# Chunk inverses of groups 0 to 5 from 16 by 16 blocks, with fillers for lone stages and a higher fill limit

## The chip, the cores and the metric

The kernel runs on one core of one Trainium2 chip. The metric is the device time in microseconds of one execution, median of several runs. A core has five engines that work side by side and wait for each other by semaphores: TensorE (PE in the profile; its weight loads are PEld), VectorE (DVE), ScalarE (ACT), GpSimd (POOL) and SyncE (SP), which issues the DMAs. TensorE writes to PSUM, eight banks of 128 partitions by 512 fp32 numbers.

## The reference

Delta-rule attention over 4 batches, 8 heads, 768 steps, head size 48, and then a gated MLP with a mixing matrix over the sequence:

```python
for t in range(S):
    y[:, :, t] = einsum('bhd,bhde->bhe', q[:, :, t], state)
    v_old = einsum('bhde,bhd->bhe', state, kt)
    state = state + bt * einsum('bhd,bhe->bhde', kt, vt - v_old)
h = relu(x @ w_in); u, v = h[..., :512], h[..., 512:]
v_n = (v - mean(v)) / sqrt(var(v) + 1e-6)
out = (u * (einsum('ts,bsd->btd', w_spatial, v_n) + b_spatial)) @ w_out
```

## The kernel before, in words

**Chunks and stages.** The sequence is cut into 12 chunks of 64 steps per batch: 48 chunk stages in an order written in `step_order` (all of batch 0, then batch 1, then two batches in turn). Each treats 8 heads, two by two on the upper and lower 64 partitions. Within a chunk the recurrence is solved in closed form, which needs the inverse of a 64 by 64 unit triangular matrix for each head. Four stages make a group, so 12 groups hold 384 inverses.

**Making an inverse.** For a group, `kk` multiplies keys with keys on TensorE and masks the product into `ta` on VectorE; `bounce` writes `ta` to DRAM (`ad`), and the diagonal blocks come back with one block per partition (`la`). There VectorE eliminates row by row, one multiply (into `prod`) and one add (into `w`, held in a PSUM tile `pw`) per row. Groups 1 to 11 do that for 32 by 32 blocks (`load_la`, `lanes`: 30 rows, 60 VectorE instructions, lines 670 and 677), and the result returns over DRAM (`wd`) into `ta`. Group 0 does it for 16 by 16 blocks (`lanes16`: 14 rows, 28 instructions, lines 1181 and 1188, all in an SBUF buffer `ub`); `widen` then makes 32 by 32 inverses of them: a transpose on VectorE (line 1208), 16 small matmuls (line 1215), a masked copy on ScalarE, 16 small matmuls (line 1226), four ScalarE copies, for each stage of the group. The step from 32 to 64 is taken for every stage by `step_t` (transpose into `tn`) and `step_ef` (two stage matmuls named e and f here, one on the diagonal quadrants).

**The chain of a stage.** `step_ab`: a (keys times state) and b (inverse times corrected values), followed on VectorE by `us`; `step_c`: the state's update, followed on VectorE by `st`; then the next stage's a, followed by `kv`. `step_qk` and `step_d` make the output. Each of these TensorE stages is 8 small fp32 matmuls on quarters of the array (the profile shows 16 records), of kind "anti" or "diag" by the quarters it uses. Two stages of different kinds can be interleaved and run at the same time, in two PSUM banks.

**The MLP.** Matmuls of 256, 384 or 512 columns in four task kinds (v, u, g, o), which become possible as chunks are done; the mixing over the sequence (g) needs all of a batch.

**What sets the order.** All engines' queues are written ahead by a planner, `Line`. It keeps an estimated time for each engine and picks the next operation by readiness and due time, with costs that are constants of the code. Where its TensorE would idle, `keep_warm` adds matmuls of a matrix of ones (256 columns, line 1282) as long as the columns of the last 3.4 us stay under `FILL` (5000). Where a stage has no partner, `fake` adds a filler stage of the other kind, made of `mpos` matrices, if the same sum is under `FAKE` (5500) and a bank is free. Nothing reads the fillers' results.

Of the kernel before, what the change touches and what calls it, by code (L numbers as in the profile page):

```python
# [15 lines left out]
CH = 64  # L16
# [3 lines left out]
G = 4  # L20
# [19 lines left out]
HOLD = 1.0  # L40
PAIR = 1.0
LOW = 3600
HOT = 3050
FILL = 5000
FAKE = 5500


def step_order():
# [196 lines left out]
def delta_rule_gated_mlp(  # L245
# [113 lines left out]
    class Slots:  # L359
# [12 lines left out]
        def ready_for(self, kind):  # L372
            f = self.fit(kind)
            return f[0][0] if f else None

        def ready_both(self):
# [270 lines left out]
    def load_la(g):  # L647
        d = due(4 * g - 7)
        src = ad_g[g].rearrange("j h n t -> (h n) j t")
        for blk in range(2):  # L650
            for par in range(2):
                l0, r0 = par * 64 + blk * 32, blk * 32
                t = yield dma(at(("ad", g), ("lanes", g - 2) if g > 2 else None), d, 4.2)
                nc.sync.dma_start(out=las[g % 2][l0 : l0 + 32], in_=src[:, r0 : r0 + 32, r0 : r0 + 32])
        done["la", g] = t

    def lanes(g):
# [2 lines left out]
        w = pws[g % 2].rearrange("p (i t) -> p i t", t=32)  # L660
        for par in range(2):
            pr = rows_t(par)
            t = yield act(at(("la", g), ("wo", g - 2) if g > 2 else None), d, 512)
            nc.scalar.copy(out=w[pr], in_=la[pr, par::2, :])  # L664
        for j in range(1, 31):
            n = (j + 1) // 2
# [8 lines left out]
            )  # L675
            t = yield dve(on(t), d, n * m)
            nc.vector.tensor_add(out=w[:, :n, j + 1 : 32], in0=w[:, :n, j + 1 : 32], in1=pr)  # L677
        done["lanes", g] = t
# [4 lines left out]
        t = yield act(both(on(t), at(("wd", g - 1) if g > 1 else None)), d, 512)  # L683
# [13 lines left out]
        done["T", g] = t  # L697


    def prev(s, n=1):  # L700
# [29 lines left out]
            done["S", s] = 0.0  # L730

    def step_t(s):
        done["t", s] = yield dve(at(("T", s // G) if s >= G else ("T", 0, s), ("e", s - 2) if s >= 2 else None), due(s - 1.1), 128)
        nc.vector.transpose(out=tns[s % 2], in_=t_of(s)[:, :, 0:32])

    def step_ef(s):
# [422 lines left out]

    extra = []  # L1160

    def lanes16():
        d = due(-6)
        buf = ubs[2]
        la = buf[:, 0:256].rearrange("p (j t) -> p j t", t=16)
        w = buf[:, 256:512].rearrange("p (j t) -> p j t", t=16)
        pt = buf[:, 512:768]
        pi = buf[:, 768:1024].rearrange("p (s u t) -> p s u t", u=NU, t=16)
        src = ad_g[0].rearrange("j h n t -> (h n) j t")
        sq = [(slice(k * 32, k * 32 + 32), src[:, k * 16 : k * 16 + 16, k * 16 : k * 16 + 16]) for k in range(4)]  # L1170
        for p, x in sq:
            t = yield dma(at(("ad", 0)), d, 2.5)
            nc.sync.dma_start(out=la[p], in_=x)
        done["la16"] = t
        t = yield act(on(t), d, 256)
        nc.scalar.copy(out=w, in_=la)
        for j in range(1, 15):
            m = 15 - j
            pr = pt[:, : j * m].rearrange("p (a b) -> p a b", b=m)
            t = yield dve(on(t), d, j * m)  # L1180
            nc.vector.tensor_tensor(
                out=pr,
                in0=w[:, :j, j : j + 1].broadcast_to([128, j, m]),
                in1=la[:, j, j + 1 : 16].unsqueeze(1).broadcast_to([128, j, m]),
                op=ALU.mult,
            )
            t = yield dve(on(t), d, j * m)
            nc.vector.tensor_add(out=w[:, :j, j + 1 : 16], in0=w[:, :j, j + 1 : 16], in1=pr)
        t = yield dve(on(t), d, 16)
        nc.vector.memset(w.rearrange("p i t -> p (i t)")[:, 0:256:17], 1.0)  # L1190
        for p, x in sq:
            t1 = yield dma(on(t), d, 2.8)
            nc.sync.dma_start(out=x, in_=w[p])
        ta = ta_of(0)
        for k, (a, b) in enumerate(((0, NU), (NU, G * NU))):
            for h in range(2):
                t = yield dma(on(t1), d, 2.8)
                nc.sync.dma_start(out=flat(0)[rows_t(h), a:b], in_=ad_g[0][:, h, a:b])
            done["back", k] = t
        for s in range(G):  # L1200
            line.spawn(widen(s, buf, pi))

    def widen(s, buf, pi):
        d = due(-5 + s)
        ta = ta_of(0)
        tr = buf[:, s % 2 * 256 : s % 2 * 256 + 256].rearrange("p (u t) -> p u t", t=CH)
        t = yield dve(at(("back", min(s, 1)), ("wp", s - 2) if s > 1 else None), d, 256)
        nc.vector.transpose(out=tr.rearrange("p u t -> p (u t)"), in_=ta[:, s].rearrange("p u t -> p (u t)"))
        t = yield Op("PE", 0.7, 1.0, both(on(t), pm_s.ready), d, "full", 150)
        p = pm_s.take()  # L1210
        pp, px = (p[1][:, o : o + 64].rearrange("p (u t) -> p u t", t=16) for o in (0, 64))
        for u in range(NU):
            for q in range(4):
                r, c = q * 32, q % 2 * 32
                nc.tensor.matmul(
                    pp[r : r + 32, u], ta[r : r + 16, s, u, c : c + 32], tr[r : r + 16, u, c : c + 16],
                    start=True, stop=True,
                )
        done["wp", s] = t
        t = yield act(on(t), d, 64, 1)  # L1220
        nc.scalar.mul(out=pi[:, s], in_=pp, mul=hm)
        t = yield Op("PE", 0.45, 0.75, on(t), d, "full", 150)
        for u in range(NU):
            for q in range(4):
                r, c = q * 32, q % 2 * 32
                nc.tensor.matmul(
                    px[r : r + 16, u], pi[r : r + 32, s, u], ta[r : r + 32, s, u, c + 16 : c + 32],
                    start=True, stop=True,
                )
        for q in range(4):  # L1230
            r, c = q * 32, q % 2 * 32
            t = yield act(on(t), d, 64)
            nc.scalar.copy(out=ta[r : r + 16, s, :, c + 16 : c + 32], in_=px[r : r + 16])
        pm_s.give(p, t)
        done["T", 0, s] = t

    def load_beta():
        done["ball"] = yield dma(now, due(-11.5))
# [2 lines left out]
    def load_bias():  # L1241
        r = slice(0, 66)
        x = ubs[2][:, 0:256]
        t = yield pool(at(("T", 0, G - 1)), due(2), 256)
        nc.gpsimd.memset(x, 0.0)
        for j in range(3):
            t = yield dma(on(t), due(2))
# [24 lines left out]
    def steps(s):  # L1272
        for f in (load_kv, step_t, step_ef, step_ab, step_c, step_qk, step_d):
# [113 lines left out]
```

## Time and profile before

| | us |
|---|---|
| median of 3 runs | 563.35 (563.08 to 565.36) |
| profiled execution | 559.02 |
| its span, first to last instruction | 557.3 |
| busy: TensorE, VectorE, ScalarE, GpSimd | 509.1, 355.2, 216.9, 140.7 |
| mean granted TensorE clock | 0.941 |

The slices of the page show when the engines are busy (tenths; 40 slices of 13.9 us) and what clock TensorE was granted:

```profile
PE 5965797978979999899999999999999999999997
DVE 4899978776977988478989894683135241134210
PEclk9777586897999999899999999999999999999999
```

TensorE is busy throughout the second half; in the first ten slices it has gaps and part of the time half clock, and VectorE is busy for most of the first 24 slices. Fillers count as busy time of TensorE. The median of the runs is 4.3 us above the profiled execution.

### The profile page before, as it was taken

The page shows a single profiled execution, that of the slowest core. Times are in us where ns is not written, and L with a number is a line of the kernel's source. Part 1 is how long each engine was busy: PE and PEld are TensorE (multiplying, and loading weights), DVE is VectorE, ACT ScalarE, POOL GpSimd, SP SyncE. Part 2 cuts the span into 40 slices and gives each one's busy share as a digit, 9 for nine tenths or more (in the row PEclk, how much of TensorE's full clock was granted, in tenths as well). Part 3 has the DMA queues.
Part 4 walks back from the last instruction along what each step waited for, and adds up shares of the span by engine and source line. Part 5 has one row for each costly group of instructions (what it writes and reads, how often), then busy time and mean ns, then how long its engine had stood idle before and what let it go on. Part 6 is the DMA issues. An engine that isn't in the chain of part 4 may idle for free.

```text
span 557.3 us, 22530 instructions
## 1 busy us (share of the span) xinstructions
PE 509.1 (91%) x9605; PEld 460.0 (83%) x9605; DVE 355.2 (64%) x1436; ACT 216.9 (39%) x536; POOL 140.7 (25%) x210
## 2 busy tenths in 40 slices
PE   5965797978979999899999999999999999999997
PEld 5855786867867879798987789989987999999997
DVE  4899978776977988478989894683135241134210
ACT  3222524544625535242235465422165441137111
POOL 5525224555425441402314252310001000000000
PEclk9777586897999999899999999999999999999999
DMA  8688378495759754786875727343014010100011
GB/s 241 163 179 163 88 186 220 113 259 104 181 158 191 187 135 91 177 219 146 204 133 79 204 73 173 112 142 62 29 35 133 8 36 29 35 18 16 1 42 44
DMA packets 134256, 67.03 MB, mean 120 GB/s; under 512 B 105894, under 2 KB 123532, under 8 KB 134156
## 3 DMA queue, kind: packets, MB, share of 16 engines
q1 hardware_dynamic: 134156, 65.60, 47.8%
q8 instruction: 75, 1.23, 0.9%
q14 instruction: 25, 0.20, 0.1%
HBM read 50.11 MB, written 15.17 MB: 117 GB/s over the span
## 4 chain that ended last, share of the span: by engine, by line
PE 65%; DVE 16%; DMA 7%; issue 4%; ACT 3%; SPq 3%; POOL 0%; DVEq 0%; ACTq 0%
PE pt L438 22%; PE pm L1044 12%; PE pw L1044 6%; PE pm L1012 6%; PE pm L946 5%; PE pm L1099 5%; PE pw L1099 3%; DVE prod L670 3%; DVE pw L677 3%; DMA kv<-in_kv_t 2%; DMA la<-ad 2%; PE pm L1282 2%; PE pw L946 2%; PE pw L1012 1%; DMA ad<-ta 1%
## 5 line engine op out<-in xcount | busy, mean ns | idle before, releaser
L670 DVE TENSOR_TENSOR prod<-pw,la 128x96 f32<-128x96 f32 (+10 forms) x330 | 78.3, 241 | 13.4 <-ACT pw L664 8.8
L677 DVE TENSOR_TENSOR pw<-pw,prod 128x96 f32<-128x96 f32 (+9 forms) x330 | 81.1, 249 | 4.6
L719 POOL TENSOR_TENSOR kv<-kv,cn 128x192 f32<-128x192 f32 x48 | 24.9, 519 | 159.4 <-DMA kv<-in_kv_t 93.1
L1044 PE MATMUL pm<-wsp_h,vh 128*128 128x256 f32 x192 | 57.0, 297 | 0.0
L1044 PE MATMUL pm<-wsp_l,vh 128*128 128x256 f32 x192 | 54.2, 282 | 0.6 <-issue 0.6
L1044 PE MATMUL pm<-wsp_h,vl 128*128 128x256 f32 x192 | 54.0, 281 | 0.0
L438 PE MATMUL pt<-kv,st 48*64 48x64 f32 x768 | 53.8, 232 | 0.0
L438 PE MATMUL pt<-aq,us 64*64 64x64 f32 x768 | 52.0, 227 | 0.8 <-issue 0.8
L438 PEld LDWEIGHTS pt<-kv,st 48*64 48x64 f32 x768 | 43.3, 142 | 3.2 <-DVE ta L630 1.5
L1080 ACT CAST gh<-tmp 128x512 fp32r<-128x512 f32 x24 | 14.8, 619 | 76.0 <-DVE tmp L1061 76.0
L438 PEld LDWEIGHTS pt<-aq,us 64*64 64x64 f32 x768 | 43.5, 142 | 1.0 <-issue 1.0
L1282 PE MATMUL pm<-ones 128*128 128x256 f32 x215 | 40.6, 339 | 3.2 <-ACT ones L282 2.5
L438 PE MATMUL pt<-ta,pi 64*64 64x32 f32 x768 | 36.2, 235 | 5.1 <-issue 3.9
L595 POOL TENSOR_TENSOR mc<-mpos,cn 128x256 f32<-128x256 f32 x46 | 28.3, 628 | 43.1 <-DVE cn L583 24.8
L438 PE MATMUL pt<-kv 48*64 48x64 f32 x768 | 36.0, 233 | 3.2 <-issue 2.2
L438 PEld LDWEIGHTS pt<-kv,ta 64*64 64x64 f32 x768 | 30.2, 145 | 9.8 <-issue 3.2
L438 PEld LDWEIGHTS pt<-st,kv 48*64 48x64 f32 x704 | 26.9, 141 | 13.8 <-issue 3.7
L1282 PEld LDWEIGHTS pm<-ones 128*128 128x128 f32 x215 | 33.8, 231 | 5.3 <-ACT ones L282 2.5
L868 ACT ACTIVATE xs<-pt 112x256 f32<-112x256 f32 x48 | 18.3, 381 | 50.7 <-PE pt L438 40.1
L1044 PEld LDWEIGHTS pm<-wsp_h,vh 128*128 128x128 f32 x192 | 36.4, 190 | 1.6
L438 PE MATMUL pt<-kv,ta 64*64 64x48 f32 x768 | 35.9, 233 | 1.9 <-DVE kv L779 0.5
L1044 PEld LDWEIGHTS pm<-wsp_h,vl 128*128 128x128 f32 x192 | 36.6, 190 | 0.6 <-issue 0.6
(182 smaller groups left out, 1488.2 us busy)
## 6 DMA issues: line engine op xcount, KB each, us to landing
kv<-in_kv_t SPq DMA_DIRECT2D x48, 456.0 KB, 4.5
ad<-ta SPq DMA_DIRECT2D x24, 256.0 KB, 4.5
la<-ad SPq DMA_DIRECT2D x44, 128.0 KB, 4.1
out<-ob SPq DMA_DIRECT2D x24, 192.0 KB, 1.9
k<-in_kv_t SPq DMA_DIRECT2D x20, 224.0 KB, 3.6
knn<-in_k_nat SPq DMA_DIRECT2D x10, 384.0 KB, 3.9
wd<-w SPq DMA_DIRECT2D x22, 128.0 KB, 3.9
ta<-wd SPq DMA_DIRECT2D x44, 64.0 KB, 3.5
```

Source lines behind the costliest of these rows:

```text
L438: return lambda: nc.tensor.matmul(*a, **dict(dict(start=True, stop=True), **k))
L595: (nc.vector if t in (0, 2) else nc.gpsimd).tensor_tensor(out=mc, in0=mall, in1=cns[t // G][:, t % G, 1].unsqueeze(2).broadcast_to([128, N ...
L670: nc.vector.tensor_tensor(out=pr, in0=w[:, :n, j : j + 1].broadcast_to([128, n, m]), in1=la[:, j, j + 1 : 32].unsqueeze(1).broadcast_to([1 ...
L677: nc.vector.tensor_add(out=w[:, :n, j + 1 : 32], in0=w[:, :n, j + 1 : 32], in1=pr)
L719: nc.gpsimd.tensor_tensor(out=v, in0=v, in1=cns[s // G][:, s % G, 0].unsqueeze(2).broadcast_to([128, NU, HD]), op=ALU.mult)
L868: nc.scalar.mul(out=xt[0:112, :, qt * 64 : qt * 64 + 64], in_=psl(held[0][1], CH)[0:112], mul=-1.0)
L946: nc.tensor.matmul(p[1], a[:, kt, ts], w[:, kt, DH:], start=(n == 0), stop=(n == 3 * NK - 1))
L1012: nc.tensor.matmul(pu[:, k], w[:, kt, d0 : d0 + 128], a[:, kt], start=(n == 0), stop=(n == 3 * NK - 1))
L1044: nc.tensor.matmul(pg[:, k], v[:, d0 : d0 + 128], w[:, si, ts], start=(n == 0), stop=False)
L1080: nc.scalar.copy(out=gh[:, hs], in_=gt)
L1099: nc.tensor.matmul(p[1][:, :DM], a[:, dd, ts], w[:, dd], start=(n == 0), stop=(n == 3 * ND - 1))
L1282: nc.tensor.matmul(free[0].rearrange("p (n t) -> p n t", t=128), ones, ones.unsqueeze(1).broadcast_to([128, 2, 128]), start=True, stop=True,)
```

## The change

Three things change together.

1. Groups 0 to 5 take their inverses from 16 by 16 blocks (`LG = 6`). `lanes16` and `widen` become functions of the group. `w` now lies in PSUM (`pw`), is copied to an SBUF tile by ScalarE and goes back to DRAM from there; `la`'s buffer also serves as the scratch space of `widen`, so the loads of group g wait until group g-2 has been widened (`laf`). From group 1 on, `widen` treats two stages at once (`WN = 2`), and it takes its PSUM bank from the four of the stages (`st_s`) instead of the MLP's (`pm_s`).
2. `FAKE` goes from 5500 to 99999: every lone stage takes a filler stage along where a bank is free.
3. `FILL` goes from 5000 to 7500.

```diff
+LG = 6
+WN = 2
+WP, WX = 0.35, 0.25
-FILL = 5000
-FAKE = 5500
+FILL = 7500
+FAKE = 99999
...
-                t = yield dma(at(("ad", g), ("lanes", g - 2) if g > 2 else None), d, 4.2)
+                t = yield dma(at(("ad", g), ("laf", g - 2) if g > 1 else None), d, 4.2)
...
-    def lanes16():
-        d = due(-6)
-        buf = ubs[2]
+    def lanes16(g):
+        d = due(4 * g - 3.5 if g else -6)
+        flat_l = las[g % 2].rearrange("p j t -> p (j t)")
+        la = flat_l[:, 0:256].rearrange("p (j t) -> p j t", t=16)
+        pt = prods[g % 2]
+        w = pws[g % 2][:, 0:256].rearrange("p (j t) -> p j t", t=16)
+        wc = ws.rearrange("p i t -> p (i t)")[:, g % 2 * 256 : g % 2 * 256 + 256].rearrange("p (j t) -> p j t", t=16)
...
         for p, x in sq:
-            t = yield dma(at(("ad", 0)), d, 2.5)
+            t = yield dma(at(("ad", g), *free), due(4 * g - 7) if g else d, 4.2 if g else 2.5)
             nc.sync.dma_start(out=la[p], in_=x)
...
+        t = yield act(both(on(t), at(("wd", g - 2) if g > 1 else None)), d, 256)
+        nc.scalar.copy(out=wc, in_=w)
...
+    def widen(g, s, n):
+        d = due(4 * g - 2 + s if g else -5 + s)
+        ta = ta_of(g)[:, s : s + n]
+        area = las[g % 2].rearrange("p j t -> p (j t)")
...
-        t = yield Op("PE", 0.7, 1.0, both(on(t), pm_s.ready), d, "full", 150)
-        p = pm_s.take()
+        t = yield Op("PE", WP * n, WP * n + 0.3, both(on(t), st_s.ready_plain), d, "full", 150)
+        p = st_s.take_plain()
...
-        if g:
+        if g >= LG:
             line.spawn(load_la(g))
             line.spawn(lanes(g))
         else:
-            line.spawn(lanes16())
+            line.spawn(lanes16(g))
```

The planner turns this into another order on every engine. In counts of the whole program: TensorE's `ones` fillers 253 before, 468 now; `mpos` filler matmuls 232 and 472; widening matmuls 128 and 768; VectorE's row steps of the inverses 688 and 528. In the rows below the numbers behind names tell buffers of the same kind apart.

VectorE before, between the inverse of group 2 and stage 8's `us` (`pw_210` is group 3's array, `ta_179` group 2's inverse):

```order
L670 TENSOR_TENSOR prod_184<-pw_210,la_182 128x110
L677 TENSOR_TENSOR pw_210<-pw_210,prod_184 128x11x10
L670 TENSOR_TENSOR prod_184<-pw_210,la_182 128x99
L734 STREAM_TRANSPOSE tn_175<-ta_179 128x128
L677 TENSOR_TENSOR pw_210<-pw_210,prod_184 128x11x9
L734 STREAM_TRANSPOSE tn_176<-ta_179 128x128
L670 TENSOR_TENSOR prod_184<-pw_210,la_182 128x96
L677 TENSOR_TENSOR pw_210<-pw_210,prod_184 128x12x8
L670 TENSOR_TENSOR prod_184<-pw_210,la_182 128x84
L677 TENSOR_TENSOR pw_210<-pw_210,prod_184 128x12x7
L562 TENSOR_REDUCE ss_198<-knn 128x8
L795 TENSOR_TENSOR us_113<-pt_203,cs_194 128x192
```

VectorE of the change where the same two arrays meet (the `us` is stage 6's; line 1237 is the transpose of `widen`, line 1208 ends an elimination):

```order
L1208 MEMSET pw_210 128x16
L1237 STREAM_TRANSPOSE la_181<-ta_179 128x512
L979 TENSOR_SCALAR sm_163<-sm_163 128x1
L985 TENSOR_SCALAR sm_163<-sm_163 128x1
L991 RECIPROCAL sm_163<-sm_163 128x1
L993 SCALAR_TENSOR_TENSOR sm_163<-sm_163 128x1
L997 RECIPROCAL sm_163<-sm_163 128x1
L999 TENSOR_TENSOR sm_163<-sm_163 128x1
L750 STREAM_TRANSPOSE tn_175<-ta_179 128x128
L750 STREAM_TRANSPOSE tn_176<-ta_179 128x128
L811 TENSOR_TENSOR us_113<-pt_204,cs_193 128x192
```

Group 3's elimination, which stood around stage 8's first steps, now ends ahead of stage 6's `us`, and group 2's inverse is ready for `tn` there.

TensorE of the change ahead of stage 6's b, with the widening of group 2 between MLP matmuls and fillers (lines 1245 and 1257 are `widen`, 1319 the `ones` filler, 962 and 1028 the MLP, 453 a stage):

```order
L1319 MATMUL pm_208<-ones 128x256
L1245 MATMUL pt_206<-la_181,ta_179 32x16 x32
L962 MATMUL pm_208<-win_h,xh 128x512 x3
L962 MATMUL pm_208<-win_l,xh 128x512 x3
L1257 MATMUL pt_206<-ta_179,la_181 16x16 x32
L1245 MATMUL pt_205<-la_181,ta_179 32x16 x32
L962 MATMUL pm_208<-win_h,xl 128x512 x3
L1319 MATMUL pm_207<-ones 128x256
L1257 MATMUL pt_205<-ta_179,la_181 16x16 x32
L1028 MATMUL pm_207<-xh,win_h 128x256 x3
L1028 MATMUL pm_207<-xh,win_l 128x256 x3
L453 MATMUL pt_204<-kv_167,ta_178 64x48
```

Before, no widening stood behind the first stage's b; each of these four blocks of 32 is new there.

TensorE around stages 13 and 14, before: stages that stand alone and fillers between them.

```order
L438 MATMUL pt_206<-kv_168 64x64 x8
L438 MATMUL pt_204<-kv_168,ta_180 64x48 x8
L1282 MATMUL pm_207<-ones 128x256 x10
L438 MATMUL pt_203<-kv_169 64x64 x8
L438 MATMUL pt_205<-us_116,kv_168 64x48 x8
L1282 MATMUL pm_207<-ones 128x256 x3
```

The same place in the change:

```order
L453 MATMUL pt_205<-st_112,kv_168 64x48
L453 MATMUL pt_206<-mpos 64x48
L453 MATMUL pt_205<-st_112,kv_168 64x48
L453 MATMUL pt_206<-mpos 64x48
L1319 MATMUL pm_207<-ones 128x256 x6
L453 MATMUL pt_203<-kv_168,ta_180 64x48
L453 MATMUL pt_206<-mpos 64x48
```

The lone stages now alternate with `mpos` fillers, and more of the gaps between them hold `ones`.

More of the change, by code (lines that the diff above doesn't have):

```diff
@@ L374, in ready_for, with plain, ready_plain, take_plain @@
             return f[0][0] if f else None
+        def plain(self):
+            return sorted(f for f in self.free if f[1] not in self.tag)
+        def ready_plain(self):
+            f = self.plain()
+            return f[0][0] if f else None
+        def take_plain(self):
+            f = self.plain()[0]
+            self.free.remove(f)
+            return f[1:]
         def ready_both(self):
@@ new lines, in lanes16 @@
+            t1 = yield dma(on(t), d, 4.0 if g else 2.8)
+            nc.sync.dma_start(out=x, in_=wc[p])
+        done["wd", g] = t1
+        ta = ta_of(g)
+        for k, (a, b) in enumerate(((0, NU), (NU, G * NU)) if g == 0 else ((0, G * NU),)):
+            for h in range(2):
+                t = yield dma(on(t1), d, 4.0 if g else 2.8)
+                nc.sync.dma_start(out=flat(g)[rows_t(h), a:b], in_=ad_g[g][:, h, a:b])
+            done["back", g, k] = t
+        n = 1 if g == 0 else WN
+        for s in range(0, G, n):
+            line.spawn(widen(g, s, n))
@@ L1230, in widen @@
         for q in range(4):
             r, c = q * 32, q % 2 * 32
[L1232 to L1235, printed above, removed]
+            t = yield act(on(t), d, 64 * n)
+            nc.scalar.copy(out=ta[r : r + 16, :, :, c + 16 : c + 32], in_=px[r : r + 16])
+        st_s.give(p, t)
+        for k in range(n):
+            done["Ts", 4 * g + s + k] = t
+        left_w[g] = left_w.get(g, G) - n
@@ L1237, in load_beta @@
+        if left_w[g] == 0:
+            done["laf", g] = t
+    left_w = {}
     def load_beta():
```

87 lines of the change are left out of this document (40 added, 47 removed).

## The prediction

> **What bounds the kernel now.** I read the page's first parts, then the same execution in three stretches, cut where the first chunk stage and the thirty-first reach VectorE (rows `us`, at 62.9 and 311.5 us), and last the waits inside the middle stretch.
>
> ```profile
> PE 509.1 (91%) x9605; PEld 460.0 (83%) x9605; DVE 355.2 (64%) x1436; ACT 216.9 (39%) x536; POOL 140.7 (25%) x210
> PE 65%; DVE 16%; DMA 7%; issue 4%; ACT 3%; SPq 3%; POOL 0%; DVEq 0%; ACTq 0%
> q8 instruction: 75, 1.23, 0.9%
> 0.00:62.90 62.90, 43.01 (x962) 39.31 (x964) 52.42 (x193) 20.82 (x59) 27.64 (x69) 0.77 0.75 173
> 62.90:311.50 248.60, 225.14 (x5174) 198.98 (x5173) 202.11 (x901) 106.08 (x270) 91.33 (x114) 0.93 0.68 163
> 311.50:557.30 245.80, 240.99 (x3474) 221.73 (x3474) 100.65 (x344) 90.03 (x208) 21.73 (x28) 1.00 0.23 64
> ```
>
> Columns of the last three: length, busy time of PE, PEld, DVE, ACT, POOL, granted clock, DMA share, GB/s. In the last stretch, C, TensorE is busy 241.0 of 245.8 us at full clock: it is the bound. In the middle one, B, TensorE idles 23.5 us, its clock is 0.93, and VectorE is busy 81%. In the first, A, VectorE is busy 83% and TensorE waits for the first inverses. What can shrink lies in A and B.
>
> ```profile
> L677 DVE TENSOR_TENSOR pw<-pw,prod 128x29 f32<-128x29 f32 (+17 forms) x250 | 60.7, 248 | 2.9
> L670 DVE TENSOR_TENSOR prod<-pw,la 128x96 f32<-128x96 f32 (+12 forms) x249 | 58.5, 240 | 8.1 <-ACT pw L664 4.9
> PE pt L438 <- issue: 11.3, 9, 3.5
> PE pt L438 <- DVE tn L734: 2.9, 4, 1.5
> PE pt L438 <- DVE pw L677: 1.5, 2, 1.3
> PE pm L1282 <- issue: 0.7, 1, 0.7
> PE pm L1044 <- issue: 0.6, 1, 0.6
> ```
>
> Of VectorE's 202.1 us in B, 119.2 are the inverse's row steps. Of TensorE's 23.5 us idle, 12.6 are "issue": the instruction itself was late. The other 10.9 wait for engines, with the inverse (`tn`, `pw`) first.
>
> Not all busy time is work. Three prices, at full clock:
>
> ```profile
> 27.57 2.66 PE L1282 MATMUL pm<-ones 128*128 128x256 f32 x20
> 543.54 2.15 PE pm L1044 x18
> 122.31 0.66 PE L438 MATMUL pt<-ta,pi 64*64 64x32 f32 x16
> 405.20 0.96 PE L946 MATMUL pw<-win_h,xh 128*128 128x512 f32 x3
> 406.69 0.85 PE L946 MATMUL pw<-win_h,xl 128*128 128x512 f32 x3
> 26.48 0.22 PE L438 MATMUL pt<-k 48*64 48x64 f32 x1
> 26.63 0.38 PE L1282 MATMUL pm<-ones 128*128 128x256 f32 x1
> 26.95 0.27 PE L438 MATMUL pt<-k 48*64 48x64 f32 x1
> ```
>
> A filler or a 256-column matmul takes 0.12 us of the queue (2.15 / 18; the 20 fillers less the last one's tail agree). A 512-column one takes (406.69 - 405.20) / 6 = 0.25. A lone stage, 8 instructions seen as 16 records, takes 0.66 less its tail of 0.21, so 0.056 per slot; a pair of stages fills the same slots. A change from stage rows to full rows costs 0.15 (26.48 to 26.63); I put both directions at 0.2. The lone stage with fillers from 26.95 to the 20 fillers at 27.57 takes 0.62 against 0.66 - 0.21 + 0.15 = 0.60, so a filler stage costs 0.02.
>
> With these, B's queue before holds 81 fillers, 408 matmuls of 256 columns, 90 of 512, 72 of 384 (0.175 each, by their columns), 1456 slots, 67 changes: 9.7 + 49.0 + 22.5 + 12.6 + 81.5 + 13.4 = 188.7 us. B lasts 248.6, so 60 us are not instructions: 23.5 idle, about (1 - 0.93) x 248.6 x 225.1 / 248.6 = 15.8 of slow clock, and some 20 of waits too short to show as gaps.
>
> **The change, priced.** All counts are from the two orders.
>
> *Added to TensorE in B.* Fillers 81 to 149: +68 x 0.12 = +8.2. 512-column matmuls 90 to 108, moved here from C: +4.5. Stage slots 1456 to 1384: -4.0. Changes 67 to 96: +5.8. Filler stages, 120 instructions or 15 stages more: +0.3. The widening of groups 1 to 5, 640 small matmuls:
>
> ```profile
> 51.06 0.62 PE L1215 MATMUL pm<-ub,ta 16*32 16x16 f32 x32 [5.74 <-DVE ub L1208]
> 53.20 0.41 PE L1226 MATMUL pm<-ta,ub 32*16 32x16 f32 x32
> 47.80:75.10 27.30, 20.84 (x629) 18.75 (x632) 23.52 (x105) 12.29 (x42) 9.22 (x14) 0.50 0.57 122
> ```
>
> Without their tails (0.21 and 0.18) that is 0.41 and 0.23 us for 16 instructions each, 0.020 a piece, and the last row says at half clock. At full clock the trace has none: between 0.010 and 0.020. I take 0.015: +9.6 (6.4 to 12.8). Sum in B: +24.4.
>
> *Taken from VectorE.* A 16-row inverse has 28 steps instead of 60.
>
> ```profile
> L1181 DVE TENSOR_TENSOR ub<-ub 128x14 f32<-128x14 f32 (+6 forms) x14 | 3.9, 282 | 0.4
> L1188 DVE TENSOR_TENSOR ub<-ub 128x14 f32<-128x14 f32 (+6 forms) x14 | 3.5, 251 | 0.3
> L1208 DVE STREAM_TRANSPOSE ub<-ta 128x256 f32<-128x256 f32 x4 | 1.6, 430 | 0.3 <-PE pm L1215 0.3
> ```
>
> Group 0's 28 steps took 7.4 us with their data in SBUF, some of 0.6 us instead of 0.2; steps on PSUM (L670, L677) never exceed 0.30. The changed kernel keeps this array in PSUM, so about 28 x 0.2 = 5.6 us. Per group: 60 x 0.244 = 14.6 becomes 5.6, plus transposes of 4 x 0.43 = 1.7, so 7.3 saved, 37 over five groups, about 20 of it in B (498 row steps there become 400).
>
> *What this buys in B.* The waits for inverses: the changed order has the transposes of groups 1, 2, 3, 4 and 5 behind the `us` of stages 0, 5, 7, 14 and 17 (first stage is 0), while the groups begin at stages 4, 8, 12, 16 and 20. So groups 1 to 3 arrive early, 4 and 5 barely. I take 9 of the 10.9 us (4 to 10.9). The clock:
>
> ```profile
> 88.80:102.40 13.60, 12.01 (x234) 10.04 (x234) 8.93 (x39) 6.17 (x15) 6.91 (x8) 0.50 0.51 136
> 126.30:133.10 6.80, 6.26 (x160) 5.98 (x162) 3.56 (x22) 3.34 (x9) 1.88 (x2) 0.50 0.34 68
> 142.00:228.00 86.00, 77.23 (x1854) 67.57 (x1852) 72.64 (x345) 41.87 (x111) 33.62 (x46) 1.00 0.64 165
> ```
>
> All half-clock time but 3.4 us of B lies before 133 us, where lone stages leave short gaps; where more full matmuls run (142 to 228) the clock stays up. The fill makes the early part like the later one: 15 of 15.8 us back (7 to 15.8). Of the 20 us of short waits I give 7 (0 to 12): a stage's steps on VectorE queue behind fewer row steps (216 rows between `us` 0 and 8 become 166).
>
> *What it costs beside.* TensorE's instructions grow by 215 + 2 x 240 + 2 x 640 = 1975 records, and as many weight loads; 75 packets for 2 x 9605 instructions is one per 256, so 15 more packets. B before has 2 x 5174 / 256 = 40 packets and 12.6 us of issue idle, 0.31 each; 15 more would be +4.7 if every one falls into work, but some fall into fillers. I take +3 (0 to 12).
>
> [...]
>
> SyncE gets a new wait: the loads of group g's blocks wait until group g-2 has been widened, since the widening now uses their buffer. For group 2 this is the end of group 0's widening, close to the first stage; behind it on the queue stand the return of group 1, the bias, `wstage` and the next `kv`. `kv` has slack of a stage, so I price it 0, up to +4 if a landing of 4 to 5 us falls onto stage 2. ScalarE gets 46 instructions of some 0.25 us, 11 us on an engine that is 39% busy: nothing, unless they hold a widening bank.
>
> B: 24.4 - 9 - 15 - 7 + 3 = **-3.6**.
>
> *A.* Group 0's row steps 1.8 us shorter, one ScalarE copy of 0.4 more, and a part of the half clock before 62.9 us (0.77 granted) gone, 2 us: **-3.5** (-7 to +4; the 81 added fillers stand in gaps of over 5 us, as the 5.74 before the first widening). *C.* Fillers 36 to 102: +7.9; 18 fewer 512-column matmuls: -4.5; 16 slots and a change less, 14 filler stages more: -0.8. Of the 4.8 us idle some 1.3 takes fillers: **+1.3** (-1 to +4).
>
> Sum: -3.6 - 3.5 + 1.3 = -5.8. The profiled execution took 559.0 us (its span is 557.3 plus 1.7 around it), the median of the runs is 563.35: 4.3 more. I apply the difference to the median: **557.5 us**.
>
> **Rivals.** *No net change, 562 us.* Stage to stage, the chain goes TensorE, VectorE three times; where no inverse is missing it may keep its pace, so the short waits stay: -5.8 + 7 = +1, or with half of it -2. For: groups 4 and 5 are planned just in time. Against: 81% of VectorE in B.
>
> *Slower: instruction fetch, 572 us.* One gap of 3.51 us at 123.33 has nothing but "issue" behind it, and a half clock follows (126.30 to 133.10). The widening brings 128 instructions (weight loads among them) in about half a microsecond, and a filler stage doubles a lone stage's count. If each of the 15 added packets stalls 1.2 us rather than 0.2, that is +15: 557.5 + 15 = 572.5. It decides from 0.6 us per packet on, where the gain of 5.8 is gone and more.
>
> *Slower: the clock stays low, 574 us.* From 88.8 to 102.4 TensorE was busy 12.0 of 13.6 us and still ran at half clock. If filling short gaps does not lift it, the 15 us of B and 2 of A do not come back: 557.5 + 17 = 574.5. For: that row. Against: the 142 to 228 row. [...]
>
> *More gain, 545 us.* All waits for inverses, all 12 us of short waits and the lower widening price, with no fetch cost: -2 - 5 - 3 - 3 on top, 557.5 - 13.
>
> **How the numbers follow.** Forecast 0.42, more gain 0.07, no change 0.20, fetch 0.20, clock 0.11. A measurement of this kernel tells 0.5%, 2.8 us. So faster 0.49, same 0.20, slower 0.31. The forecast's own range is 549 to 560.5; to leave out no more than 2 in 10 it must reach up into the slow rivals: 545 to 573, with the upper halves of the two slow rivals outside.
>
> **What would show it.** Right: granted clock near 1.0 in all slices after the first few; first `us` near 59 us and thirty-first near 304; no wait for `tn` or `pw` in the first twenty stages; 28 row steps of 0.2 us per group. Wrong: "issue" well over 20 us on TensorE (fetch); half-clock slices before 133 us (clock); the thirty-first `us` after 312 with the clock up (chain pace); C longer than 250 us (fillers that displace work).

## The result, and the profile after

| | before | after |
|---|---|---|
| median, us | 563.22 (557.88 to 565.36) | 596.35 (594.83 to 600.84) |
| ratio | | 1.062 [1.052, 1.071] |
| span of the profiled execution, us | 557.3 | 593.5 |
| stretch A (to the first `us`) | 62.9 | 59.0 |
| stretch B (to the thirty-first `us`) | 248.6 | 284.3 |
| stretch C | 245.8 | 250.2 |

The change makes the kernel 6% slower; the forecast was 557.5, faster. Both medians are from four runs taken side by side. Runs that lie more than 1.5% above the fastest of their kernel count as disturbed and are left out of each ratio, while a median is of all runs; where this leaves one run (e6_fill), no ratio is given.

The first parts of the page after, then its stretches A, B and C (columns as in the prediction: length, busy time of PE, PEld, DVE, ACT, POOL, granted clock, DMA share, GB/s).

```profile
PE 557.8 (94%) x11580; PEld 504.1 (85%) x11580; DVE 335.7 (57%) x1280; ACT 227.4 (38%) x582; POOL 141.0 (24%) x211
PEclk9986657975998967999999999989999999999999
q8 instruction: 91, 1.49, 1.0%
PE 80%; DVE 6%; issue 5%; DMA 5%; SPq 2%; ACT 1%; POOL 0%; ACTq 0%; DVEq 0%; POOLq 0%
```

```profile
0.00:59.00 59.00, 50.37 (x1070) 46.72 (x1072) 46.34 (x174) 19.41 (x57) 26.93 (x69) 0.88 0.72 179
59.00:343.30 284.30, 262.41 (x6802) 229.19 (x6800) 197.73 (x812) 120.61 (x325) 91.46 (x115) 0.86 0.57 142
343.30:593.50 250.20, 245.05 (x3714) 228.14 (x3714) 91.68 (x295) 87.39 (x200) 22.66 (x29) 0.99 0.21 59
```

VectorE did lose work: 335.7 us instead of 355.2, and its share of the chain falls from 16% to 6%. TensorE took over the chain, 80% instead of 65%. Nearly all of the loss is in B: +35.7 of the span's +36.2 us. There TensorE's idle time is 284.3 - 262.4 = 21.9 us, hardly less than the 23.5 before, so what grew is its busy time, from 225.1 to 262.4 us, and its clock is lower, 0.86 instead of 0.93.

TensorE's waits in B after (what it waited for, total us, times, longest):

```profile
PE pt L1257 <- issue: 7.8, 6, 3.5
PE pt L453 <- issue: 5.4, 5, 2.5
PE pt L1245 <- issue: 2.7, 2, 2.4
PE pt L1245 <- DVE la L1237: 1.0, 1, 1.0
PE pt L453 <- DVE pw L1206: 0.7, 1, 0.7
PE pt L453 <- DVE tn L750: 0.2, 1, 0.2
```

The waits for the inverse are nearly gone (`tn` and `pw` 0.2 + 0.7 us, from 2.9 + 1.5). In their place stand 15.9 us of "issue", idle time in which the profile shows nothing to wait for (late instructions, below), where it was 12.6; 10.5 of them lie inside the two lines of the widening (L1245, L1257), which also waits 1.0 us for its own transpose; in the state stages late instructions fell from 11.3 to 5.4 us.

What the added matmuls took: the ones fillers in B before, then in B and in C after, then the two halves of the widening in B after (length, PE busy, PEld busy, clock, DMA share, GB/s).

```profile
62.90:311.50 248.60, 15.81 (x81) 11.49 (x81) 0.93 0.68 163
59.00:343.30 284.30, 33.34 (x149) 23.84 (x149) 0.86 0.57 142
343.30:593.50 250.20, 17.41 (x102) 14.21 (x102) 0.99 0.21 59
59.00:343.30 284.30, 9.27 (x640) 8.05 (x640) 0.86 0.57 142
59.00:343.30 284.30, 8.14 (x640) 6.46 (x640) 0.86 0.57 142
```

The widening is busy for 17.4 us and stalls for 10.5 more. One such stall, in TensorE's timeline after:

```profile
125.90 0.67 PE L1257 MATMUL pt<-ta,la 32*16 32x16 f32 x62
130.06 0.23 PE L1257 MATMUL pt<-ta,la 32*16 32x16 f32 x2 [3.49 <-issue]
```

62 of the 64 records run in 0.67 us, then nothing happens for 3.5 us, with no engine to wait for, and the last two follow.

### The profile page after: what moved, and what is told of

Its sections match the earlier page's. It is cut to its first block, busy times and chain, and to the rows that moved or that the text cites. A ratio compares the mean times of both kernels' runs of the same rounds, so it can differ in the third digit from the quotient of the medians.

```text
span 593.5 us, 26389 instructions
## 1 busy us (share of the span) xinstructions
PE 557.8 (94%) x11580; PEld 504.1 (85%) x11580; DVE 335.7 (57%) x1280; ACT 227.4 (38%) x582; POOL 141.0 (24%) x211
## 4 chain that ended last, share of the span: by engine, by line
PE 80%; DVE 6%; issue 5%; DMA 5%; SPq 2%; ACT 1%; POOL 0%; ACTq 0%; DVEq 0%; POOLq 0%
PE pt L453 26%; PE pm L1060 13%; PE pm L1028 8%; PE pm L962 7%; PE pm L1319 7%; PE pm L1115 6%; PE pw L1060 5%; PE pw L1115 3%; DMA kv<-in_kv_t 2%; PE pw L962 2%; DMA ta<-ad 2%; PE pw L1028 2%; PE pt L1245 1%; PE pt L1257 1%; SPq L1221 1%
## 5 line engine op out<-in xcount | busy, mean ns | idle before, releaser
L1319 PE MATMUL pm<-ones 128*128 128x256 f32 x458 | 82.2, 317 | 2.5 <-ACT ones L285 2.5
L1319 PEld LDWEIGHTS pm<-ones 128*128 128x128 f32 x458 | 67.2, 210 | 5.9 <-ACT ones L285 2.5
L1060 PE MATMUL pm<-wsp_h,vh 128*128 128x256 f32 x204 | 59.9, 294 | 0.0
L735 POOL TENSOR_TENSOR kv<-kv,cn 128x192 f32<-128x192 f32 x48 | 24.4, 508 | 147.4 <-DMA kv<-in_kv_t 77.7
L453 PE MATMUL pt<-kv,st 48*64 48x64 f32 x768 | 57.9, 242 | 0.1
L1060 PE MATMUL pm<-wsp_l,vh 128*128 128x256 f32 x204 | 57.5, 282 | 0.0
L1060 PE MATMUL pm<-wsp_h,vl 128*128 128x256 f32 x204 | 57.4, 281 | 0.0
L453 PE MATMUL pt<-aq,us 64*64 64x64 f32 x768 | 55.4, 237 | 1.3 <-issue 1.3
L685 DVE TENSOR_TENSOR prod<-pw,la 128x120 f32<-128x120 f32 (+10 forms) x180 | 43.6, 244 | 7.8 <-ACT pw L679 3.9
L692 DVE TENSOR_TENSOR pw<-pw,prod 128x120 f32<-128x120 f32 (+9 forms) x180 | 45.2, 253 | 4.2
L1077 DVE TENSOR_TENSOR tmp<-pm,ub 128x512 f32<-128x512 f32 x17 | 11.8, 691 | 49.3 <-PE pm L1063 49.0
```

What stands on the lines that cost most here:

```text
L453: return lambda: nc.tensor.matmul(*a, **dict(dict(start=True, stop=True), **k))
L685: nc.vector.tensor_tensor(out=pr, in0=w[:, :n, j : j + 1].broadcast_to([128, n, m]), in1=la[:, j, j + 1 : 32].unsqueeze(1).broadcast_to([1 ...
L735: nc.gpsimd.tensor_tensor(out=v, in0=v, in1=cns[s // G][:, s % G, 0].unsqueeze(2).broadcast_to([128, NU, HD]), op=ALU.mult)
L1060: nc.tensor.matmul(pg[:, k], v[:, d0 : d0 + 128], w[:, si, ts], start=(n == 0), stop=False)
L1319: nc.tensor.matmul(free[0].rearrange("p (n t) -> p n t", t=128), ones, ones.unsqueeze(1).broadcast_to([128, 2, 128]), start=True, stop=True,)
```

## The experiments

A difficulty runs through them. The planner writes all queues ahead, and each rule that is changed gives another order. Some runs therefore differ by their order as well as by what they were made for. I tell them first, and then those that keep the order and change only what stands in it.

### One edit without the other

Only the fillers (blocks for group 0 alone), only the blocks (fillers as before), and blocks for three groups of six:

```diff
-LG = 6
+LG = 1
```

> The changed kernel with 32 by 32 blocks from group 1 on again, so that only the fillers differ from the kernel before (467 ones and 696 filler matmuls instead of 253 and 232). Theory W (the widening is the cause: its dense small matmuls outrun instruction fetch and let the clock fall): 552 to 566 us, granted clock above 0.96, first to thirty-first us within 240 to 252 us. Rival F (the fillers are the cause, they displace work and add instructions): 585 to 600 us. Rival M (the cause is the MLP work that moved behind stage 23): 552 to 566 us as W, since 343 MLP matmuls stand ahead of stage 23 here as before.

```diff
-FILL = 7500
-FAKE = 99999
+FILL = 5000
+FAKE = 5500
```

> The changed kernel with both fill limits as before (5000 and 5500): 192 ones and 200 filler matmuls, the 16 by 16 blocks kept. W: as slow as the changed kernel or slower, 592 to 610 us, clock at or below 0.92, half-clock windows beginning within a widening. F: back to 550 to 566 us. M: 585 to 600 us, since only 227 MLP matmuls stand ahead of stage 23.

```diff
-LG = 6
+LG = 3
```

> The changed kernel with 16 by 16 blocks in groups 0 to 2 only: two of the five new widenings stay. W: about two fifths of the loss, 570 to 580 us, half clock around the widenings of groups 1 and 2 only (before 125 us). F: 585 to 600 us. M: 552 to 566 us, since 428 MLP matmuls stand ahead of stage 23, more than before.

| kernel | us | ratio to before |
|---|---|---|
| fillers only (e1_lg1) | 582.47 | 1.039 [1.034, 1.045] |
| blocks only (e2_blocks) | 583.96 | 1.045 [1.037, 1.053] |
| fillers, three groups (e3_lg3) | 585.06 | 1.045 [1.038, 1.052] |

Each edit alone loses some 20 us, so no theory that put the whole loss on one edit stands: 582 for the fillers alone is far from the 552 to 566 of those that blame the blocks, and 584 for the blocks alone is far from the 550 to 566 of the one that blames the fillers. Theory M, which put the loss on MLP matmuls that moved behind stage 23, had 552 to 566 for the first and the third run and falls with them.

One matmul of 256 columns after every eight small ones of the widening, to keep the clock up:

```diff
+def keep():
+    nc.tensor.matmul(warm, ones, ones.unsqueeze(1).broadcast_to([128, 2, 128]), start=True, stop=True)
 ...
+                if g and u % 2:
+                    keep()
```

> The changed kernel with one ones filler after every 8 small matmuls of the widenings of groups 1 to 5 (80 more, 9.6 us at full clock), written to the unused half of the same bank. W: the clock holds better and fetch has more time, granted clock 0.94 or more, and the time falls in spite of the fillers, to 575 to 588 us. M and F: 600 to 608 us, 596 plus the added fillers, clock unchanged near 0.92.

633.01 us, 1.130 [1.123, 1.137], worse than any theory. What the 80 added matmuls took (duration min, median and max in ns), and how late the widening's instructions were then:

```profile
L1243 PE MATMUL pt<-ones x80: 382/582/582, 64.4 to 260.8; 128*128 128x256 f32 x80
PE pt L1264 <- issue: 0.6, 1, 0.6
```

In the trace the next small matmul starts 0.31 us after such a matmul of 0.39 us, and the one before it starts 0.11 earlier: 0.42. Where they last 0.582 us instead of 0.382, an estimate is 0.20 more, 0.62. So 80 of them take 80 x 0.42 to 0.62 = 34 to 50 us by this estimate; the loss against the changed kernel is 37. A filler between small tiles costs not 0.12 us but 0.4 to 0.6; 0.12 and two changes of shape at 0.15 make 0.42, so these changes are the likely reason, which no run shows by itself. The stalls of the widening all but vanish (0.6 us instead of 10.5); why is not shown. The clock did not rise: it is 0.80 in B of this run, against 0.86 in the changed kernel.

### The fillers

On the base with group 0 alone from blocks: that base itself, then one filler rule at a time, then no filler.

```diff
-LG = 6
-FILL = 7500
-FAKE = 99999
+LG = 1
+FILL = 5000
+FAKE = 5500
```

> The changed kernel with 16-row blocks for group 0 alone and the old rules for both fillers (5000 columns, 5500): the base from which the runs on fillers and on bursts differ by one thing each. All theories: 558-568.

The next three differ from it in one or two constants: `FAKE = 99999`, then `FILL = 7500`, then both at 0.

> The changed kernel with 16-row blocks for group 0 alone, the old fill (5000 columns) and a filler stage with every lone state stage: 640 filler-stage matmuls instead of 232, the same 240 ones fillers. Theory D (each filler takes its own queue time from work): 51 more filler stages at 0.02 us, 1 us, so 562-567. Theory K (a filler stage costs far more than its slots, by the bank it holds or by the fetch of its instructions): 573-585. Theory G (the 20 us of the run with group 0 alone and both fillers come from the ones fillers): 560-567, as D.

> The same with the fill of 7500 columns and the old rule for filler stages: 491 ones fillers instead of 253, 48 filler-stage matmuls instead of 232. Theory D: 240 more fillers at 0.12 us are 29 us, of which what falls into real gaps is free; with two thirds displacing work 578-588. Theory K: the ones fillers sit in gaps and cost little, 560-570.

> The same with no filler of either kind (group 0 alone from 16-row blocks). Theory D carried through: fillers cost more than the clock they keep, 545-563. The other theory, that the 250 fillers of the kernel before hold the clock up and only the additional ones are too many: half clock over most of the first 300 us, 590-640.

And the kernel before itself, with fewer fillers (`FILL = 0`, `FAKE = 0`; `FILL = 3500`, `FAKE = 0`; `FAKE = 0` alone):

> The kernel before with no filler of either kind, nothing else changed. Theory D (fillers cost their queue time and their clock saves no time, since stages wait for one another, not for the clock): 550-562. Theory H (the fillers of the kernel before earn their place through the clock): 568-590.

> The kernel before with a fill of 3500 columns instead of 5000 and no filler stages: 104 ones fillers instead of 253. Theory D: between the kernel before and the one without fillers, 552-563. Theory H: 563-575.

> The kernel before without filler stages, its ones fillers kept (249). Theory D: a filler stage costs next to nothing beside its lone stage, 560-565. If filler stages cost through their instructions: 552-560.

| kernel | us | ratio to before |
|---|---|---|
| base, group 0 from blocks (c0_g0) | 571.67 | 1.014 [1.008, 1.021] |
| base, all filler stages (e5_fake) | 576.55 | 1.024 [1.018, 1.031] |
| base, fill of 7500 (e6_fill) | 579.2 (567.35 to 580.77) | none given |
| base, no fillers (e7_nofill) | 565.23 | 1.007 [1.003, 1.012] |
| before, no fillers (b1_nofill) | 559.31 | 0.995 [0.991, 0.999] |
| before, fill of 3500, no filler stages (b3_fill3500) | 567.83 | 1.011 [1.007, 1.014] |
| before, no filler stages (b2_ones_only) | 575.31 | 1.023 [1.018, 1.028] |

The base was expected at 558 to 568 and came out at 571.67. Its first stages tell why: the `us` rows of the first five stages (duration min, median and max in ns, first and last start), before and then in the base, and SyncE's issue of group 1's loads in the same two.

```profile
L795 DVE TENSOR_TENSOR us<-pt,cs x5: 347/357/358, 62.9 to 90.8; 128x192 f32<-128x192 f32 x5
48.12 3.48 SPq L654 DMA_DIRECT2D la<-ad  x3
```

```profile
L811 DVE TENSOR_TENSOR us<-pt,cs x5: 349/357/358, 61.9 to 101.7; 128x192 f32<-128x192 f32 x5
58.89 2.21 SPq L669 DMA_DIRECT2D la<-ad  x3
```

In the base the planner put these loads behind loads of weights and bias on SyncE's queue, which wait 5.3 us for VectorE and 2.0 for GpSimd; they go out 10.8 us later, and the fifth stage comes 10.9 us later. In these two runs the order of one queue is worth some 10 us. The three runs on the kernel before say the same in another way: no fillers is a little faster, fewer fillers is slower, no filler stages is slower still, and no price per filler gives that series. Theory D holds for the first, H for the second and neither for the third. So differences of 10 us between these seven kernels can't be put down to fillers. What they do show is that the best of them has none at all: without the 253 ones and 232 filler-stage matmuls, and in the order that comes of it, the kernel before is as fast as with them (0.995). What the fillers are worth in one order these runs can't tell.

Without fillers TensorE still runs at half speed around 100 us. In the run with group 0 from blocks and no fillers, two sets of three matmuls of 512 columns there:

```profile
99.39 1.65 PE L962 MATMUL pm<-win_h,xh 128*128 128x512 f32 x3
100.83 1.48 PE L962 MATMUL pm<-win_l,xh 128*128 128x512 f32 x3
```

(100.83 - 99.39) / 3 = 0.48 us each, twice the 0.25 of full speed. The trace of that kernel has no record of the clock before 103 us, so the page's clock of its first slices is not a reading, and these durations are. The same holds for the kernel before without fillers, whose record begins at 101 us, so its clock in B isn't known.

### The fillers alone, in the changed kernel's own order

The planner counts the fillers, but they are not issued, and every queue is otherwise the same.

```diff
 def idle(t):
     free = ...
-    if free:
-        nc.tensor.matmul(free[0]..., ones, ones..., start=True, stop=True)
     return bool(free)
 def fake(kind, t, n):
     ...
-    return (r * 2)[:n]
+    return [lambda: None] * n
```

> The changed kernel with every queue in the same order, but neither kind of filler matmul issued (the planner still counts them). So only their time and their effect on the clock go, and the order, which moved between all other runs on fillers, stays. If the fillers displace work: 570-585. If they earn their time through the clock: 590-605.

592.32 us, 1.056 [1.048, 1.065], against 1.062 [1.052, 1.071] with them: not told apart, in the range expected if the fillers earn their time. Its stretches B and C:

```profile
60.20:347.60 287.40, 250.51 (x6187) 220.28 (x6184) 197.20 (x813) 122.64 (x328) 91.17 (x115) 0.80 0.57 141
347.60:589.20 241.60, 232.44 (x3356) 214.12 (x3356) 91.40 (x294) 86.20 (x199) 23.15 (x28) 1.00 0.22 61
```

In B the fillers raise the clock from 0.80 to 0.86 and take 15.0 us of idle time away (36.9 to 21.9). The ones are busy for 33.3 us, yet TensorE's busy time grows by only 11.9 (250.5 to 262.4), and 3.1 us are left over: 287.4 becomes 284.3. In C, where the clock is full without them (1.00), the fillers add 12.6 us of busy time (232.4 to 245.1), 0.12 for each of the 102 ones; 4.0 fall into the 9.2 us that were idle, and the stretch grows by 8.6. The forecast's price of a filler was right in C; what it buys was not.

### The widening alone

On the base, 640 small matmuls of the widening's shapes on a constant, whose results nothing reads, in the places of the widening; then, in the same order, each 32 of them as 4 matmuls of 256 columns, on the full array and on 16 rows by 32 columns of it.

```diff
+def burst(g, s, n):
+    t = yield Op("PE", WP * n, ..., "full", 150)
 ...
+    for k in range(n):
+        for u in range(NU):
+            for q in range(4):
+                nc.tensor.matmul(pp[r : r + 32, k, u], mpos[r : r + 16, c : c + 32], mpos[r : r + 16, c : c + 16], ...)
```

> Group 0 alone from 16-row blocks, old fill, old filler stages, and 640 small matmuls on a constant (the shapes and count of the widening of groups 1 to 5, in the same places, into a state bank, which nothing reads). Theory F (the burst itself costs: instructions fetched late and clock lost to quarter-array work): 577-590, with gaps of 1 to 4 us inside the bursts and more half clock before 150 us. Theory R (the 16-row blocks cost by their chain over VectorE, ScalarE and the returned loads, the matmuls only their 0.015 us each): 570-575, clock as before.

```diff
-    for k in range(n):
-        for u in range(NU):
-            for q in range(4):
-                nc.tensor.matmul(pp[...], mpos[...], mpos[...], ...)
+    for k in range(2 * n):
+        nc.tensor.matmul(out, ones, wide, ...)
```

> The run with the bursts (640 small matmuls, 598.9 us), each burst of 32 small matmuls replaced by 4 matmuls of 256 columns on the full array: the same order of all else, about the same 0.5 us of the queue, 80 instructions instead of 640. Theory I (the number of instructions, fetched late): the base plus 10 us, 570-578. Theory L (quarter-array work lets the clock fall): also 570-578, with the clock up. Theory Q (any half microsecond at these places costs several times its length, since stages wait behind it): 588-600.

```diff
-        nc.tensor.matmul(out, ones, wide, ...)
+        nc.tensor.matmul(out[0:32], ones[0:16, 0:32], wide[0:16], ...)
```

> As the last, but the 4 matmuls of 256 columns use 16 rows and 32 columns of the array: few instructions, the array all but empty. Theory I: 570-578, as on the full array. Theory L: 583-600 with more half clock than on the full array. Theory Q: 588-600.

| kernel | us | ratio to before | instruction packets |
|---|---|---|---|
| 640 small matmuls (e8_burst) | 598.9 | 1.065 [1.059, 1.070] | 85 |
| 80 wide, full array (e9_full) | 578.43 | 1.023 [1.014, 1.032] | 76 |
| 80 wide, 16 x 32 of the array (e10_quarter) | 578.88 | 1.027 [1.019, 1.035] | 76 |

Three kernels with one order, and B of each (small, wide on the full array, wide on its corner):

```profile
61.60:345.30 283.70, 245.45 (x6184) 217.71 (x6183) 212.07 (x929) 109.35 (x271) 91.10 (x113) 0.85 0.61 145
61.40:325.20 263.80, 229.77 (x5215) 202.49 (x5212) 210.95 (x930) 108.86 (x270) 91.08 (x113) 0.94 0.65 155
58.90:328.60 269.70, 243.42 (x5224) 213.49 (x5223) 212.93 (x929) 109.21 (x271) 90.84 (x113) 0.88 0.64 153
```

The run with the small matmuls lies above both ranges that were expected of it, the two with wide ones at the upper edge of theory I's. The number of instructions costs 20.5 us (598.9 - 578.4). How much of the array they fill makes 0.5 us in the medians, less than their spread, though the clock in B is 0.88 with the corner and 0.94 with the full array: theory I in the main. B itself is 5.9 us longer with the corner in these profiles (269.7 against 263.8), where (1 - clock) x busy time would give 15. Against the corner, whose clock is the nearer one, the small matmuls lengthen B by 14.0 us, and 12.0 of these are idle time of TensorE (38.3 against 26.3). Against the full array B is 19.9 us longer, but only 4.2 of these are idle; the rest is busy time, with the clock at 0.85 instead of 0.94. TensorE's late instructions in the whole execution with the small matmuls, and then with the wide ones on the full array:

```profile
PE pt L453 <- issue: 16.8, 11, 3.7
PE pt L1292 <- issue: 6.7, 4, 2.5
PE pt L1283 <- issue: 4.3, 2, 3.7
```

```profile
PE pt L453 <- issue: 12.4, 12, 1.7
```

11.0 us of stall lie within the bursts (L1283, L1292) and 4.4 more in the state stages (16.8 against 12.4); the wide ones show none of their own. The 20.5 us over 9 more packets are 2.3 us each.

Where the stalls stand says more of them. Three of them follow one another in the run with the small matmuls (first fence), and between the first and the second, and the second and the third, TensorE runs 128 matmuls and 128 weight loads (second fence: length, then busy time and count of PE and of PEld):

```profile
86.07 0.20 PE L453 MATMUL pt<-us,kv 64*64 64x48 f32 x1 [1.21 <-issue]
90.90 0.23 PE L453 MATMUL pt<-st,kv 48*64 48x48 f32 x1 [2.22 <-issue]
96.54 0.30 PE L1283 MATMUL pt<-mpos 16*32 16x16 f32 x7 [3.74 <-issue]
```

```profile
86.07:90.89 4.82, 2.60 (x128) 2.45 (x128) 1.98 (x8) 1.98 (x4) 0.75 (x1) 0.67 0.88 199
90.89:96.53 5.64, 1.90 (x128) 1.73 (x128) 4.72 (x17) 0.41 (x1) 2.60 (x4) 0.50 0.71 221
```

That is 256 instructions, the size of one packet: 2 x 9605 records over 75 packets before the change are 256 each, 2 x 11580 over 91 after it 254.5. The trace of the changed kernel has seven such gaps of over 1 us, and they stand 1, 11, 12, 5, 15 and 16 times 256 records apart, short by about one record in each 256. In the same trace one packet of the instruction queue begins 2.2 to 3.1 us before TensorE goes on, for each of the seven. This is what packets that come late would give, in the widening and in the state stages alike; that TensorE waits for just these packets is inferred from the distances and times. Most of the some 90 borders show no such gap.

The same bursts in pieces of 8 matmuls, at least 0.6 us apart in the plan:

```diff
+                if u % 2 == 0 and k + u:
+                    t = yield Op("PE", WP / 2, WP / 2 + 0.3, on(t + 0.6), d, "full", 150)
```

> The run with the bursts (598.9 us), each burst of 32 small matmuls cut into four pieces of 8 that the planner puts at least 0.6 us apart. Theory R (instructions that come faster than they can be fetched stall, so only a dense burst costs): stalls inside the pieces gone, 573-585. Theory N (every added instruction costs its fetch wherever it stands): 592-605.

581.28 us, 1.033 [1.026, 1.041]: 17.6 less than in dense bursts, with the same 640 matmuls, and 4.5 us of stall within the pieces instead of 11.0; they became fewer, not none as theory R had it. The order is another one here, so the size is not exact; the direction is that of theory R.

And the widening of the changed kernel itself, with its order kept: each burst of 32 as 3 wide matmuls of zeros and 4 of the small ones.

```diff
+        if g:
+            blank(p[1])
-        for k in range(n):
-            for u in range(NU):
+        for k in range(1 if g else n):
+            for u in range(1 if g else NU):
```

> The changed kernel with every queue in the same order, but each of the 20 bursts of 32 small matmuls (groups 1 to 5) issued as 3 matmuls of 256 columns of zeros and 4 of the small ones: about the same half microsecond undisturbed, 7 instructions instead of 32 (the inverses of these groups are then not the reference's). If late instructions are what the widening costs: 575-586. If it is the order and the chain of the blocks: 592-600.

582.65 us, 1.042 [1.037, 1.048] against 1.062 [1.052, 1.071]: 13.7 us less. Its B, its packets, and its first two waits in B:

```profile
60.40:333.50 273.10, 255.75 (x5741) 222.47 (x5739) 198.23 (x813) 120.51 (x326) 91.18 (x114) 0.91 0.61 148
q8 instruction: 82, 1.34, 1.0%
PE pt L457 <- issue: 5.7, 5, 2.5
PE pt L457 <- ACT pi L768: 3.7, 3, 1.9
```

B is 11.2 us shorter, its clock 0.91 instead of 0.86. Late instructions in B fall from 15.9 to 5.7 us, with none left in the widening. Other waits come in their place, so idle time falls by only 4.5 us (21.9 to 17.4); the other 6.7 are busy time at the higher clock. 13.7 us over 9 packets are 1.5 us a packet. Late instructions and clock move together here, and this run doesn't part them.

The last run takes all fillers from the planner (`FILL = 0`, `FAKE = 0`) and keeps the blocks:

> The changed kernel with all six groups from 16-row blocks and no filler of either kind; the run with group 0 alone and no fillers took 565.2. If the blocks cost their 20 us by themselves: 580-592. If they cost only together with fillers (fetch, clock): 560-572.

589.04 us, 1.045 [1.038, 1.053], 23.8 us above the one with group 0 alone and no fillers: the blocks, with the order that they bring, cost by themselves.

## Why the prediction was wrong

**A** was forecast at -3.5 and came out at -3.9. The row steps came as priced (medians of 197 and 203 ns after the change); the other terms of A were not measured apart, so that the sum fits is in part luck.

**The additions to B held, but for one.** With the widening in few instructions (f2_few), B is 273.1 - 248.6 = 24.5 us longer than before, and the sum of what is added was +24.4: as if the additions stood at their price and none of the savings had come. That the two agree so closely is luck, since waits and clock differ there too. The addition that didn't hold is the widening. The piece itself was well priced (0.67 us less a tail of 0.18, for 31 matmuls of two records, is 0.016). The 3 us for late instructions look right as well, since these grew by 3.3 us in B; but that is luck. The widening's own are 10.5 us, and the state stages happen to have 5.9 less. In the order of the changed kernel, the widening in few instructions takes 10.2 us of late instructions and 13.7 us of time away.

**The step that failed is "What this buys in B"**: 9 us of waits for inverses, 15 of clock, 7 of short waits. The waits for `tn` and `pw` went as forecast and came back in part as late instructions, so idle time in B fell by 1.6 us in all. What grew is busy time, by 37.3 us. The clock went down, not up: by the prediction's own formula, (1 - clock) x busy time, slow clock takes (1 - 0.86) x 262.4 = 36.7 us instead of 15.8, so +21 stands where -15 was forecast. That would be 36 of the 39 us by which B was missed. Two things pull the clock about in the runs that keep one order: small matmuls in place of wide ones on the full array lower it (0.94 to 0.85, and 0.91 to 0.86 in the changed kernel), and the fillers raise it (0.80 to 0.86), but what they give there is what they cost.

How much time a lower clock takes isn't settled. The formula takes all of it for time lost, and the runs speak against its full size: wide matmuls on the corner and on the full array differ by 0.06 of clock in B and by 5.9 us there, where the formula gives 15, and by 0.5 us in all. The 61 executions of the kernel before that were run beside these experiments say the same: 0.01 less of mean clock goes with 3 to 4 us more, where the formula, with 509 us busy, gives 5; which of the two drives the other is not shown. Why the price is lower than the formula's is argued, not shown: stage to stage the work goes from TensorE to VectorE and back, and a faster TensorE waits longer there.

**C** was forecast at +1.3 and is +4.4; in the same order, taking the fillers out makes it 8.6 shorter. The text had priced C's fillers at 7.9 and balanced them with matmuls moved to B. The sign that it named for fillers that displace work, C longer than 250 us, came (250.2).

**The rivals.** *Instruction fetch* fits the stalls of the widening (one packet of the instruction queue ahead of the end of each of seven stops), its bound "from 0.6 us per packet on" was passed with 1.5 and 2.3, of which the stalls themselves are 10.2 / 9 = 1.1 and 15.4 / 9 = 1.7, and its 1.2 a packet for 15 packets, 572, was too little. The sign that I named for it, issue well over 20 us, did not come (15.9 in B): the stalls are seen better by where they lie, in the widening's own lines and at steps of 256 instructions. *The clock stays low* was right in what it saw (half-clock slices before 133 us); its 574 was for a clock that stays at 0.93 in B, not one that falls to 0.86. *No net change* had the short waits stay; no run here measures these by themselves.

**What adds up, and what stays open.** From 596.35 the fillers' own matmuls take 4.0 (within the spread of the runs) and the widening's surplus instructions 13.7. A kernel with both taken out of the one order was not run; if they add, it is at 578.6, 15 us above before. In it are the replacements of the widening's bursts, an estimate of 20 x (3 x 0.12 + 4 x 0.015) = 8 us, and the rest, some 7 us, is the size that another order alone has shown. That rest isn't settled. Part of it could be the stage bank that the widening holds from group 1 on, which no run takes away by itself.

## What to carry to other kernels

Count instructions, not only their time: here dense bursts of tiny matmuls, half a microsecond each on paper, cost 1.5 and 2.3 us more for each packet of 256 instructions than about the same queue time in few instructions (13.7 and 20.5 us in all); in pieces at least 0.6 us apart in the plan they cost 17.6 us less, in another order. Look whether gaps with nothing to wait for stand a fixed number of instructions apart, as they do here at multiples of 256. Fillers in a queue that is written ahead cost most of their time where the clock is full anyway (8.6 of 12.6 us in C); ask first whether the time follows the clock, by running the kernel with no fillers at all. And where a planner makes the order, a change of its rules moves the time by its new order; keep the order and change only what is issued to learn what one edit costs.

## What was not expected of the hardware

- TensorE stopped for 3.49 us, with nothing in the profile to wait for, in the middle of a burst whose 62 records took 0.67 us.
- In the two traces where it was counted, TensorE's stops of over 1 us with nothing to wait for stand multiples of 256 instructions apart (to about one record in each 256), matmuls and weight loads counted together.
- Matmuls of 256 columns on 16 x 32 of the array leave the granted clock of B at 0.88, on the full array at 0.94, in one profile each; the medians of the two are 578.9 and 578.4 us.
- A matmul of 256 columns on the full array, put between small fp32 tiles, held the queue for 0.42 us, not 0.12, and by an estimate for 0.62 where it lasts 0.582 us instead of 0.382.
